# A fast matrix product whose first and fifth products get a PSUM tile each, the first in a single bank

## The chip, the cores and the metric

The kernel runs on one NeuronCore of a Trainium2 chip. The metric is device time in microseconds (us), the median of several runs; lower is better.

## The reference, cut to what matters

```python
def _attn_ref(q, k, v, proj):          # (2, 8, 768, 64) each, proj (64, 6)
    ...
    mask = q_bucket[:, :, :, None] == k_bucket[:, :, None, :]
    scores = scale * np.matmul(q, k.transpose(0, 1, 3, 2))
    scores = np.where(mask, scores, -1000000000.0)
    ...
    return np.matmul(attn, v)
def _moe_ref(x, domain_probs, w1, w2): # x (1536, 512), w1 (4, 512, 1024), w2 (4, 1024, 512)
    p = domain_probs / (domain_probs.sum(-1, keepdims=True) + 1e-09)
    for e in range(E):
        h = np.maximum(x @ w1[e], 0.0)
        out += p[:, e:e + 1] * (h @ w2[e])
```

A hashed attention of two batches is followed by a mixture of four experts on its output. The change touches only the first layer of the experts, `max(x @ w1, 0)`.

## The kernel before, in words

The expert part is cut into 16 **units**, eight for each batch of 768 rows. A unit takes one expert's 512 of 1024 hidden columns: its first layer makes the hidden values (transposed, 128 hidden columns by 384 rows at a time), its second layer multiplies them with `w2` and adds the result to an accumulator. Every fp32 operand is split into a high and a low part, and a product is three matmuls: high by high, high by low, low by high.

Units 0 to 4 use plain products (`unit`). From unit 5 on (`FAST = 5`) there are 11 **fast units** (`unit_fast`, three in batch 0, eight in batch 1). Their first layer is a Strassen-Winograd scheme: four blocks of the result from seven products instead of eight. It is done in two **halves** (`for j in range(2)`, L1096), each with seven products of six matmuls with 384 columns (`product`, L1059 to L1070; its matmuls are L1064, L1067 and L1068). In the text P1 to P7 are the products of a half in the order of the code:

- P1 (L1099) into `pa`; ScalarE then copies `pa` to SBUF as `s1` (L1100).
- P2 (L1104) into `pd`.
- P3 (L1107) into `pb`; VectorE then makes `u2 = pb + s1` and `v1 = pd + u2` (both recorded as L1094, the line of the helper `add`).
- P4 (L1111) is added onto `pa`, whose final value goes to ScalarE (`hh`, L1074) and VectorE (`hl`, L1079) as hidden values.
- P5 (L1116) into `c22`, from which VectorE makes `u3` and `c22 + v1`.
- P6 (L1121) is added onto `pd`, then `pd + u2`.
- P7 (L1127) into `c21`, then `u3 - c21` (L1128).

Each block's hidden values are again an `hh` on ScalarE and an `hl` on VectorE. In between, ScalarE and GpSimd split the `w2` weights (L1049 and L1050), and after the two halves `second_layer` runs six row tiles of 12 matmuls (L783 to L785), each drained by one VectorE instruction (L777 or L813), while the next unit's `w1` operands are made (L1004, L1008, L1013).

PSUM has two pools: `big` gives tiles of two banks (`[P, 2, 512]` fp32, 2 buffers, used by the attention scores too) and `one` gives tiles of one bank (`[P, 512]`, 4 buffers, used by nearly everything else). Before, `pa` and `pd` are the two halves of one `big` tile:

```python
            both = big("mps")
            pa, pd = both[:, 0, :SB], both[:, 1, :SB]
```

The order of instructions on each engine is the order in which the program issues them (`tc.manual_schedule()`); the attention is a generator that is advanced between the steps of the units by costs written into the `yield`s, so that order is fixed before the kernel runs. The tile framework adds the semaphore waits between engines and gives a pool's buffer to a new tile when the old tile's last user is done. In unit 5 the last head's product with `v` (`pv`, L563, in a `one` tile) still runs between P4 and P5 of the first half.

Of the kernel before, what the change touches and what calls it, by code (L numbers as in the profile page):

```python
# [55 lines left out]
def tile_lsh_attention__then__domain_moe(  # L56
# [21 lines left out]
    SB = 384  # L78
# [44 lines left out]
    def pair_tile(shape, name):  # L123
        return pp.tile(shape, F32, tag="pm", name=name, bufs=2)

    def big(name):
        return ps2.tile([P, 2, 512], F32, tag="big", name=name)

    def one(name):
        return ps1.tile([P, 512], F32, tag="one", name=name)  # L130
# [629 lines left out]
    def block(s, f):  # L760
        used = rows_h.setdefault(s, [None, FC])
        if used[1] == FC:
            used[0] = [hp.tile([P, FC, SB], F32R, tag=tag, name=tag) for tag in ("hh", "hl")]
            used[1] = 0
        used[1] += 1
        return tuple(x[:, f] for x in used[0])
# [78 lines left out]
    def drained():  # L845
        while next(att, None) is not None:
            pass
# [132 lines left out]
    def x_ops_late():  # L980
        xop.update(next_ops)
        _, b12, _, b22 = x_blocks(1)
        pair_in("t3", ((stk, "q1"), (stk, "al")))
        t3 = combine(b22, b12, ALU.subtract)
        keep(xop, "t3", t3)
        yield
# [55 lines left out]
    def split_w2_fast(g):  # L1042
        hi = wp.tile([P, KD, HALF], F32R, tag="w2hi", name="w2hi")
        lo = wp.tile([P, KD, HALF], F32R, tag="w2lo", name="w2lo")
        wts[g, 1] = (hi, lo)
        for c in range(0, KD, WC):
            t = staged.pop((g, 1, c))
            for o in range(WC):
                nc.scalar.activation(hi[:, c + o], t[:, o], ACTF.Copy)  # L1049
                nc.gpsimd.tensor_tensor(  # L1050
                    out=lo[:, c + o], in0=t[:, o], in1=hi[:, c + o].bitcast(F32), op=ALU.subtract
                )
            load_w()
            yield

    def unit_fast(b, u, first_u):
        hs = {}

        def product(ps, w, x, j, first):  # L1059
            whi, wlo = w  # L1060
            xh, xl = ([t[k] if isinstance(t, list) else t[:, k] for k in range(KH)] for t in x)
            fs = slice(j * P, (j + 1) * P)
            for kk in range(KH):
                nc.tensor.matmul(  # L1064
                    ps, whi[:, kk, fs], xh[kk], start=first and kk == 0, stop=False, skip_group_check=True
                )
                nc.tensor.matmul(ps, whi[:, kk, fs], xl[kk], start=False, stop=False, skip_group_check=True)  # L1067
                nc.tensor.matmul(  # L1068
                    ps, wlo[:, kk, fs], xh[kk], start=False, stop=kk == KH - 1, skip_group_check=True
                )  # L1070

        def hidden_hi(s, f, src):
            hh, hl = block(s, f)
            nc.scalar.activation(hh, src, ACTF.Relu)  # L1074
            hs[s, f] = (hh, hl)

        def hidden_lo(s, f, src):
            hh, hl = hs[s, f]
            nc.vector.scalar_tensor_tensor(  # L1079
                out=hl, in0=src, scalar=0.0, in1=hh.bitcast(F32), op0=ALU.max, op1=ALU.subtract  # L1080
            )

        def hidden(s, f, src):
            hidden_hi(s, f, src)
            hidden_lo(s, f, src)

        w = wts.pop((first_u + u, 0))
        sp2 = split_w2_fast(first_u + u)
        ma, mb = (pair_tile([P, 2, SB], "mt") for _ in range(2))
        s1, u2, v1, u3 = ma[:, 0], ma[:, 1], mb[:, 0], mb[:, 1]  # L1090
        c21 = None

        def add(out, ps, t):
            nc.vector.tensor_tensor(out=out, in0=ps, in1=t, op=ALU.add)  # L1094

        for j in range(2):  # L1096
            both = big("mps")
            pa, pd = both[:, 0, :SB], both[:, 1, :SB]
            product(pa, w["a11"], xop["b11"], j, True)  # L1099
            nc.scalar.activation(s1, pa, ACTF.Copy)  # L1100
            if j:
                hidden_lo(0, 1 + j, c21)
            yield 1120
            product(pd, w["s1"], xop["t1"], j, True)  # L1104
            yield 1120
            pb = one("mps")[:, :SB]
            product(pb, w["s2"], xop["t2"], j, True)  # L1107
            add(u2, pb, s1)
            add(v1, pd, u2)
            yield 1120  # L1110
            product(pa, w["a12"], xop["b21"], j, False)  # L1111
            hidden(0, j, pa)
            next(sp2, 0)
            yield 1120
            c22 = one("mps")[:, :SB]
            product(c22, w["s3"], xop["t3"], j, True)  # L1116
            add(u3, c22, u2)
            add(c22, c22, v1)
            hidden_hi(1, 2 + j, c22)
            yield 1120  # L1120
            product(pd, w["s4"], xop["b22"], j, False)  # L1121
            add(pd, pd, u2)
            hidden_lo(1, 2 + j, c22)
            hidden_hi(1, j, pd)
            yield 1120
            c21 = one("mps")[:, :SB]
            product(c21, w["a22"], xop["t4"], j, True)  # L1127
            nc.vector.tensor_tensor(out=c21, in0=u3, in1=c21, op=ALU.subtract)  # L1128
            hidden_lo(1, j, pd)
            hidden_hi(0, 2 + j, c21)  # L1130
            yield 1120
        hidden_lo(0, 3, c21)
        for _ in sp2:
            pass
        xo = None
        if b == 0 and u >= EARLY:
            drained()
            xo = early if u + 1 < NU else x_ops_late()
        yield from second_layer(b, u, first_u, hs, wts.pop((first_u + u, 1)), xo)
# [72 lines left out]
```

## Time and profile before

| | |
|---|---|
| median of 3 runs | 772.59 us (772.42 to 772.99) |
| profiled execution: time, span | 772.19 us, 770.4 us |
| busy share of the span: PE, DVE, ACT, POOL | 93%, 64%, 42%, 40% |
| matmuls | 3714 |

The span goes from the first to the last instruction of the profiled execution; about 1.8 us lie around it. PE is TensorE's matmul, PEld its weight load, DVE VectorE, ACT ScalarE, POOL GpSimd, SP the queue that starts the DMAs. Busy time of PE is a modelled figure, since matmuls are pipelined: the distance from one matmul's start to the next one's is the better measure of its pace.

### The profile page before, as it was taken

Reading aid. Unit: us, or ns where it says so; the run is one execution under the profiler, and the core shown is the slowest. Engines: PE = TensorE matmul, PEld = TensorE weight load, DVE = VectorE, ACT = ScalarE, POOL = GpSimd, SP = SyncE. Lnnn points to the kernel's source line nnn. Section 1 sums busy time; section 2 is a strip of 40 time slices with the busy share of each in tenths; the row PEclk is TensorE's granted clock in tenths of the full one; section 3 lists DMA queues with packets and bytes.
Section 4 is the critical chain, followed back from the end, with each engine's and each line's share of the span. In section 5 each row is a group of like instructions: output and inputs, shape, how many; then the busy total and the mean of one; then the engine's idle time right before and its main releaser. Section 6 shows DMA issues by size and latency. Waiting matters only on the chain. (4 is left out here: it accounts for less than half of the span.)

```text
span 770.4 us, 10205 instructions
## 1 busy us (share of the span) xinstructions
PE 714.9 (93%) x3714; PEld 587.0 (76%) x3714; DVE 494.5 (64%) x821; ACT 327.3 (42%) x640; POOL 307.8 (40%) x290
## 2 busy tenths in 40 slices
PE   8999999999999999998888888888898979797988
PEld 6767667978878888886777777777777768686876
DVE  7897988855856656565575756656564646474742
ACT  6887786525534354343333332323232323232330
POOL 6466867243524443253453533323232414141320
PEclk9999999999999999999999999999999999999999
DMA  5325235978978977875111123111112121120202
GB/s 128 73 42 128 52 97 132 246 185 235 248 225 210 231 228 205 244 242 137 54 58 56 54 69 123 55 55 55 55 54 82 47 64 57 53 82 28 83 1 82
DMA packets 90850, 87.77 MB, mean 114 GB/s; under 512 B 53168, under 2 KB 55728, under 8 KB 90800
## 3 DMA queue, kind: packets, MB, share of 16 engines
q1 hardware_dynamic: 89776, 86.80, 40.8%
q8 instruction: 29, 0.48, 0.3%
q10 hardware_dynamic: 1024, 0.33, 0.2%
q14 instruction: 21, 0.17, 0.1%
HBM read 65.04 MB, written 22.07 MB: 113 GB/s over the span
## 5 line engine op out<-in xcount | busy, mean ns | idle before, releaser
L783 PE MATMUL mps<-w2hi,hh 128*128 128x512 f32 (+1 forms) x388 | 151.0, 389 | 0.0
L785 PE MATMUL mps<-w2hi,hl 128*128 128x512 f32 (+1 forms) x388 | 150.4, 388 | 0.0
L784 PE MATMUL mps<-w2lo,hh 128*128 128x512 f32 (+1 forms) x388 | 150.3, 387 | 0.0
L1050 POOL TENSOR_TENSOR w2lo<-ws,w2hi 128x512 fp32r<-128x512 f32 x44 | 56.1, 1296 | 193.8 <-ACT w2hi L1049 110.3
L1064 PE MATMUL mps<-xo,w1hi 128*128 128x384 f32 x260 | 92.5, 356 | 33.2 <-DVE mt L1094 20.9
L1074 ACT ACTIVATE hh<-mps 128x384 fp32r<-128x384 f32 x88 | 43.3, 492 | 150.0 <-PE mps L1068 110.8
L448 DVE TENSOR_SCALAR_CACHE_REDUCE p<-sps 128x768 f32<-128x768 f32 x96 | 90.0, 939 | 17.7 <-PE sps L443 16.0
L777 DVE SCALAR_TENSOR_TENSOR acc<-mps,pe,acc 128x512 f32<-128x512 f32 (+1 forms) x85 | 63.0, 741 | 59.4 <-PE mps L785 59.1
L464 ACT ACTIVATE p<-p,nb 128x768 f32<-128x768 f32 x96 | 89.5, 932 | 23.4 <-DVE p L448 23.0
L1068 PE MATMUL mps<-xo,w1lo 128*128 128x384 f32 x260 | 87.4, 336 | 0.0
L1067 PE MATMUL mps<-xo,w1hi 128*128 128x384 f32 x260 | 87.3, 336 | 0.0
L1064 PEld LDWEIGHTS mps<-xo,w1hi 128*128 128x128 f32 x260 | 48.8, 188 | 49.4 <-DVE mt L1094 26.0
L785 PEld LDWEIGHTS mps<-w2hi,hl 128*128 128x128 f32 x388 | 72.9, 188 | 15.4
L783 PEld LDWEIGHTS mps<-w2hi,hh 128*128 128x128 f32 x388 | 72.9, 188 | 15.4 <-issue 1.2
L784 PEld LDWEIGHTS mps<-w2lo,hh 128*128 128x128 f32 x388 | 72.9, 188 | 13.8
L1094 DVE TENSOR_TENSOR mt<-mps,mt 128x384 f32<-128x384 f32 x66 | 36.8, 557 | 65.7 <-PE mps L1068 64.9
L1079 DVE SCALAR_TENSOR_TENSOR hl<-mps,hh 128x384 fp32r<-128x384 f32 x88 | 48.7, 553 | 44.6 <-ACT hh L1074 42.4
L563 PE MATMUL pv<-pt,tv 128*64 128x384 f32 x288 | 67.1, 492 | 0.0
L1008 POOL TENSOR_TENSOR w1lo<-ws,w1hi 128x512 fp32r<-128x512 f32 x33 | 45.3, 1377 | 41.5 <-issue 14.7
L831 PE MATMUL mps<-xs,w1hi 128*128 128x384 f32 x160 | 54.3, 339 | 0.0
L441 PE MATMUL sps<-ah,q 128*128 128x384 f32 x192 | 53.7, 360 | 0.4 <-DVE p L448 0.4
L833 PE MATMUL mps<-xs,w1lo 128*128 128x384 f32 x160 | 53.8, 336 | 0.0
(136 smaller groups left out, 1332.8 us busy)
## 6 DMA issues: line engine op xcount, KB each, us to landing
ws<-in_moe_w_dram SPq DMA_DIRECT2D x64, 512.0 KB, 3.9
scr<-t SPq DMA_DIRECT2D x16, 1152.0 KB, 8.0
pt<-scr SPq DMA_DIRECT2D x64, 288.0 KB, 6.0
tv<-in_v_dram SPq DMA_DIRECT2D x16, 192.0 KB, 2.9
tqk<-in_q_dram SPq DMA_DIRECT2D x30, 96.0 KB, 3.1
out_dram<-acc SPq DMA_DIRECT2D x11, 256.0 KB, 2.0
tqk<-in_k_dram SPq DMA_DIRECT2D x28, 96.0 KB, 3.3
rdb<-row SPq DMA_DIRECT2D x14, 192.0 KB, 6.5
```

The costliest lines, as they stand in the source:

```text
L448: nc.vector.tensor_scalar(out=two(pt), in0=ps[:, :, :NH], scalar1=MASKED, scalar2=MASKED, op0=ALU.min, op1=ALU.min, accum_out=nb,)
L464: nc.scalar.activation(pt, pt, ACTF.Exp, bias=nb, scale=-1.0, accum_out=dens[b, h, r][:, o : o + 1])
L563: nc.tensor.matmul(dst, vvs[b, h][:, c], pts[b, h, g][c], start=c == 0, stop=c == NT - 1, tile_position=(0, g * D),)
L777: nc.vector.scalar_tensor_tensor(out=acc, in0=ps, scalar=pcol, in1=acc, op0=ALU.mult, op1=ALU.add)
L783: nc.tensor.matmul(ps, hh[:, ts], w2hi[:, f, cs], start=n == 0, stop=False)
L784: nc.tensor.matmul(ps, hh[:, ts], w2lo[:, f, cs], start=False, stop=False)
L785: nc.tensor.matmul(ps, hl[:, ts], w2hi[:, f, cs], start=False, stop=n == FC - 1)
L831: nc.tensor.matmul(ps[:, :SB], w1hi[:, kk, fs], xhi[b, kk][:, sl], start=kk == 0, stop=False)
L1050: nc.gpsimd.tensor_tensor(out=lo[:, c + o], in0=t[:, o], in1=hi[:, c + o].bitcast(F32), op=ALU.subtract)
L1064: nc.tensor.matmul(ps, whi[:, kk, fs], xh[kk], start=first and kk == 0, stop=False, skip_group_check=True)
L1067: nc.tensor.matmul(ps, whi[:, kk, fs], xl[kk], start=False, stop=False, skip_group_check=True)
L1068: nc.tensor.matmul(ps, wlo[:, kk, fs], xh[kk], start=False, stop=kk == KH - 1, skip_group_check=True)
```

## The change

`pa` becomes a tile of one bank out of the pool `one`; `pd` is the first half of a `big` tile, whose second half is left unused. No instruction is added, removed or reordered by the diff, and no operand changes its shape.

```diff
         for j in range(2):
-            both = big("mps")
-            pa, pd = both[:, 0, :SB], both[:, 1, :SB]
+            pa, pd = one("mps")[:, :SB], big("mps")[:, 0, :SB]
             product(pa, w["a11"], xop["b11"], j, True)
             nc.scalar.activation(s1, pa, ACTF.Copy)
```

## Rows read from the trace of the kernel before

**Rows 1.** The page: instructions and busy shares, and the granted clock in 40 slices.
```profile
PE 714.9 (93%) x3714; PEld 587.0 (76%) x3714; DVE 494.5 (64%) x821; ACT 327.3 (42%) x640; POOL 307.8 (40%) x290
...
PEclk9999999999999999999999999999999999999999
```

**Rows 2.** Busy time by stretch: fast units' first layers, without unit 5's 364.53:368.55.
```profile
core 0: us, PE busy (x) PEld busy (x) DVE busy (x) ACT busy (x) POOL busy (x), PEclk, DMA share, GB/s
356.53:364.53 8.00, 4.83 (x26) 3.94 (x24) 4.79 (x8) 1.76 (x3) 1.66 (x1) 1.00 0.98 242
368.55:381.94 13.39, 11.37 (x62) 10.41 (x61) 7.72 (x15) 4.71 (x10) 2.24 (x2) 1.00 0.11 39
...
730.07:750.43 20.36, 16.21 (x85) 14.29 (x84) 9.52 (x18) 6.25 (x13) 4.79 (x4) 1.00 0.00 1
sum 226.47, PE 178.28 PEld 157.26 DVE 109.68 ACT 69.69 POOL 57.93; mean PE 14.86 PEld 13.10 DVE 9.14 ACT 5.81 POOL 4.83
```

**Rows 3.** Busy time by stretch: attention beside plain units, and one second layer.
```profile
120.00:344.70 224.70, 224.70 (x1185) 187.28 (x1184) 149.47 (x248) 101.40 (x199) 93.92 (x87) 1.00 0.82 221
...
713.73:730.07 16.34, 16.34 (x74) 13.52 (x73) 12.09 (x16) 4.96 (x9) 5.49 (x5) 1.00 0.29 98
```

**Rows 4.** Line L1064, whole span: what PE and PEld together waited for.
```profile
  DVE mt L1094: 64.3, 44
  ACT mt L1100: 40.5, 44
  DVE hl L1079: 9.5, 21
```

**Rows 5.** Timeline of PE, last first layer: first matmuls of P1, P2, P3, P4, P6, P7, P1.
```profile
730.07 0.34 PE L1064 MATMUL mps<-xo,w1hi 128*128 128x384 f32 x1
...
731.91 0.44 PE L1064 MATMUL mps<-xo,w1hi 128*128 128x384 f32 x1 [0.64 <-ACT mt L1100]
...
733.06 0.34 PE L1064 MATMUL mps<-xo,w1hi 128*128 128x384 f32 x1
...
735.58 0.45 PE L1064 MATMUL mps<-xo,w1hi 128*128 128x384 f32 x1 [1.31 <-DVE mt L1094]
...
738.06 0.45 PE L1064 MATMUL mps<-xo,w1hi 128*128 128x384 f32 x1
...
739.21 0.34 PE L1064 MATMUL mps<-xo,w1hi 128*128 128x384 f32 x1
...
740.25 0.34 PE L1064 MATMUL mps<-xo,w1hi 128*128 128x384 f32 x1
```

**Rows 6.** Timeline of ACT, the same first layer.
```profile
731.37 0.49 ACT L1100 ACTIVATE mt<-mps 128x384 f32<-128x384 f32 x1 [3.66 <-PE mps L1068]
736.92 0.49 ACT L1074 ACTIVATE hh<-mps 128x384 fp32r<-128x384 f32 x1 [5.07 <-PE mps L1068]
737.31 1.14 ACT L1049 ACTIVATE w2hi<-ws 128x512 fp32r<-128x512 f32 x2
```

**Rows 7.** Timeline of DVE, around the same first layer.
```profile
728.22 0.68 DVE L1008 TENSOR_TENSOR w1lo<-wc,w1hi 128x512 fp32r<-128x512 f32 x1
730.27 0.75 DVE L777 SCALAR_TENSOR_TENSOR acc<-mps,pe,acc 128x512 f32<-128x512 f32 x1 [1.37 <-PE mps L785]
734.37 1.15 DVE L1094 TENSOR_TENSOR mt<-mps,mt 128x384 f32<-128x384 f32 x2 [3.35 <-PE mps L1068]
737.45 0.56 DVE L1079 SCALAR_TENSOR_TENSOR hl<-mps,hh 128x384 fp32r<-128x384 f32 x1 [1.92 <-ACT hh L1074]
...
751.11 1.20 DVE L1079 SCALAR_TENSOR_TENSOR hl<-mps,hh 128x384 fp32r<-128x384 f32 x2
```

**Rows 8.** Timeline of POOL, second half of the same first layer.
```profile
748.19 2.54 POOL L1050 TENSOR_TENSOR w2lo<-ws,w2hi 128x512 fp32r<-128x512 f32 x2 [7.57 <-ACT w2hi L1049]
```

**Rows 9.** Timeline of SP at the start of unit 5.
```profile
354.95 1.79 SPq L545 DMA_DIRECT2D pt<-scr  x4
```

**Rows 10.** DMA issues, 354.9 to 366.5 us: count, KB each, median us to landing.
```profile
pt<-scr SPq DMA_DIRECT2D x4, 288.0 KB, 6.0
```

## The prediction, made before the changed kernel ran

> **What bounds the kernel now.** I read the page first: PE is busy 93% of the span and its granted clock is at the upper level, 2.4 GHz, in all 40 slices [rows 1]. So TensorE is the bound, and a change can gain no more than the time in which TensorE stands still. The view by stretch says where that is. Between 120 and 344.7 us PE is busy 100% of the time, and in a second layer it is too: 16.34 of 16.34 us [rows 3]. The first layers of the fast units are different: the last one takes 20.36 us with 16.21 busy, and the eleven together take 226.47 us, without the 4.02 us that the attention's last `pv` product takes out of unit 5 [rows 2].
>
> What the stops wait for stands in the view of the line of the products' first matmul: VectorE's additions 44 times, ScalarE's copy `s1` 44 times, `hl` 21 times [rows 4]. PE and its weight load are counted apart there, so that is 22 stops each (11 units by 2 halves) behind the additions and the copy, and 21 behind `hl`. The timeline shows which products stop [rows 5]. P7 starts at 739.21 and the next P1 at 740.25, so a product that nothing holds up takes 1.04 us and a half of seven would take 7.28. It takes 740.25 − 730.07 = 10.18. The 2.90 us too many lie so:
>
> - P1 to P2: 1.84 us instead of 1.04. P2 starts at 731.91; the copy of `pa` ends at 731.37 + 0.49 = 731.86 [rows 6].
> - P2 to P3: 1.15, so 0.11 more after the restart.
> - P3 to P4: 2.52, so 1.48 more. P4 starts at 735.58; the pair `u2`, `v1` ends at 734.37 + 1.15 = 735.52 [rows 7].
> - P4 to P6: 2.48 instead of 2.08, so 0.40, of which 0.11 is P4's restart. P6 starts at 738.06; `hl` of `pa` ends at 737.45 + 0.56 = 738.01 [rows 7].
> - P6 to P7: 1.15, again 0.11 of restart.
>
> Each stop ends 0.05 or 0.06 us after an instruction on the *other* half of the tile `both`. P2 writes `pd` and waits for a reader of `pa`; P4 writes `pa` and waits for `v1`, which reads `pd`; P6 writes `pd` and waits for `hl`, which reads `pa`. None of the three pairs shares a value. I conclude that waits are kept for the tile as a whole.
>
> **The change part by part.** It adds and removes no instruction. With `pa` and `pd` in two tiles, P2 has nothing to wait for but its buffer; P4 must wait only for the copy of `pa`, P6 only for `v1`.
>
> *The gain.* Eleven first layers of 14.56 us are 160.16, against 226.47: 66.31 us [rows 2, 5].
>
> *What comes late next.* I lay a half out anew, P1 at 0. A reader starts 1.31 us after its product's first matmul (734.37 − 733.06) [rows 5, 7]. Copy `s1`: 1.31 to 1.80, and P4 starts at 3.12. `u2` and `v1`: P3 at 2.08, so 3.39 to 4.54; P6 starts at 5.20 and needs `v1`, with 0.6 us to spare. ScalarE's `hh` of `pa` is at 4.43, its weight pair ends at 4.43 + 0.39 + 1.14 = 5.96 [rows 6], `hl` of `pa` starts at 4.96 (737.45 − 736.92 later). Behind it come seven more VectorE instructions of about 0.56 us, some waiting for P5, P6 and P7 and for `hh`: `u3` at 5.47, `c22 + v1` until 6.5, its `hh` until 7.0 and its `hl` until 7.6; carried on, 9.3 for the last `hl`. The next half's `u2` is due at 7.28 + 3.39 = 10.67, and VectorE is busy only 9.52 us in a first layer [rows 2]. So no product waits, and I cost the rest of the half at nothing; if `v1` came late after all, the wait at P6 returns, up to its present 0.40 a half, 8.8 us in all.
>
> *The second layer* starts at 14.56. GpSimd's second pair of `w2lo` runs 748.19 to 750.73 [rows 8]; P4 of that half started 735.58 + 10.18 = 745.76, so in the new half, with P4 at 10.40, it ends at 15.37. The last piece is wanted at about 14.56 + 7 matmuls of 16.34 / 72 = 0.227 us [rows 3], 16.15: 0.8 us to spare. The weight load that waits for it goes out 0.5 us later against the second layer than before; the next unit's last operand is done 1.2 us before P1 now (728.22 + 0.68 against 730.07) [rows 3, 7] and is wanted by P6, so I take nothing for that.
>
> *Buffers.* P1 now draws from the four `one` tiles: 14 a unit instead of 12. If they go round in turn, P1 of the second half gets the buffer of the first half's `pa`, free at 5.5, and P1 of a unit that of the second layer's third row tile, long drained. Nothing.
>
> *Unit 5.* After P4, at 356.53 + 4.16 = 360.69, comes `pv` instead of at 364.53 [rows 2]. Its `pt` loads were issued until 354.95 + 1.79 = 356.74 [rows 9] and land 6.0 us later by the median [rows 10], 362.74. So it would wait: 0 at the least, 3.84 at the most (it ran at 364.53 before); I take 2.1 from the landing. The `pv` tile also stands in the ring of `one` tiles, and in turn its buffer falls to P3 of the second half. Its two copies come behind `s1`: at like shapes [rows 6, 7] 1.80 + 0.49 + 0.56 = 2.85 after P1 against 2.08, with the restart 0.9 us. Bounds are 0 and 0.9, since the ring is only my reading; I take 0.9.
>
> *Sum*: 66.3 − 2.1 − 0.9 = 63.3 us. From the profiled execution 772.19 − 63.3 = 708.9; its median is 0.4 above it, so 709.3.
>
> *A rule against it.* The rows say that P2 waits for a reader of another half of its tile. The Trainium skill ("PSUM — Partial Sum Buffer", section "PSUM bank collisions raise a hardware error") has engines kept apart by bank and quadrant; two halves of 512 fp32 are two banks, so by that rule nothing between them would have had to wait, the change would remove no wait, and the time would stay at 772.6. The trace disagrees with it as a description of this program: 22 stops behind the copy.
>
> **The rivals.**
>
> 1. *The stop is not the shared tile's*, and stays: 772.6. For it: `hl` of SBUF tiles is tracked in parts (the second layer begins at 750.43 [rows 2] while VectorE writes other parts of the same `hl` at 751.11 [rows 7]), so tiles need not be tracked whole. Against it: three stops a half, each 0.05 us after a reader of the other half of `both`, and no other instruction ends there. 6%.
>
> 2. *Too few one-bank buffers*: P1 gets a buffer freed late. The latest that can be meant are, at the unit's start, the sixth row tile, whose drain ends at 731.02 [rows 7], 1.0 us after P1's start, and, in the second half, `c22`, whose `hl` ends at 7.6 in the layout above, 0.4 after P1's 7.28. With 0.11 of restart each that is 1.6 us a unit, 17.6 in all: 727. Against it: a second layer takes its six row tiles from the same ring, and PE never stops in it [rows 3]. 7%.
>
> 3. *Slower: the clock.* If TensorE without its stops fell to its lower level, 1.2 GHz, in the first layers, each would cost 14.56 us more. From 63.3 / 14.56 = 4.3 of the eleven on this eats the gain; with all eleven the time is 709.3 + 160 = 869. Against it: 224.7 us without a stop at a granted clock of 1.00 [rows 3]. 2%.
>
> 4. *P6 keeps its wait* because VectorE runs behind: 709.3 + 8.8 = 718. It lies inside the forecast's range.
>
> **How the numbers follow.** The forecast, including number 4, has 85%. Its own range goes from 706.3 (all of the 66.3 us: 772.6 − 66.3) to 718. I widen it by a microsecond at each end, 705 to 719, which leaves out rivals 1 to 3 (15%) and some odd case. About 0.2% is what a measurement here can tell from no change. Faster: 85 + 7 = 92%; the same 6%; slower 2%.
>
> **What would show it.** By stretch, first layers of 14.6 us in batch 1 and second layers of 16.3 still; on L1064 no idle time behind `s1`, the additions or `hl` beyond a few us; PE busy near 99%. A stop at P6 behind the additions would say that `v1` is late, one at P1 behind L777 or `hl` that the ring is too small, one before `pv` in unit 5 that `pt` had not landed. The prediction is wrong if P2 still starts 0.05 us after the copy, or if a new stop appears at the second layer's first row tile.

## The result and the profile after

| | before | after |
|---|---|---|
| median of 4 runs | 772.50 us | 712.18 us (710.60 to 713.37) |
| ratio, 95% interval | | 0.9217 (0.9198 to 0.9237) |
| profiled execution: time, span | 772.19, 770.4 us | 713.37, 711.6 us |

The changed kernel is 7.8% faster. The forecast of 709.3 us was 2.9 us too low, with the time inside its range. (The "fifth" product of the title is P2 in the numbering of the text: `pd` takes P2, and P6 is added onto it.)

The page of the changed kernel, its parts on busy time and on the granted clock:

```profile
PE 701.8 (99%) x3714; PEld 592.3 (83%) x3714; DVE 498.6 (70%) x821; ACT 327.7 (46%) x640; POOL 307.7 (43%) x290
...
PEclk9999999999999999999999999999999999999999
```

Beside [rows 1], the work is the same, 3714 matmuls, and PE has gone from 93% to 99% of a span that is 58.8 us shorter. Of these, 45.7 us are idle time of TensorE (770.4 − 714.9 before, 711.6 − 701.8 after). The other 13.1 are modelled busy time around the stops: before a stop a matmul counts its whole 0.34 us, and behind one 0.44, while in a run only 0.17 us lie between two starts.

Busy time by stretch in the changed kernel: unit 5's first layer up to the end of P4, its `pv` part and its rest; the first layers of units 6, 7 and 8 and the last one, the sum of these and the seven in between, and a second layer. The columns are those of [rows 2].

```profile
358.02:362.34 4.32, 4.32 (x25) 3.99 (x23) 4.25 (x8) 1.76 (x3) 1.68 (x1) 1.00 0.85 200
362.34:371.61 9.27, 6.62 (x26) 2.76 (x25) 1.06 (x2) 1.64 (x3) 2.50 (x2) 0.82 0.65 172
371.61:382.17 10.56, 10.56 (x62) 10.56 (x62) 7.72 (x15) 4.72 (x10) 1.85 (x2) 1.00 0.12 44
398.53:413.43 14.90, 14.89 (x85) 14.57 (x84) 11.44 (x20) 6.99 (x14) 7.41 (x6) 1.00 0.17 57
429.79:444.46 14.67, 14.67 (x85) 14.59 (x84) 10.75 (x19) 6.34 (x14) 8.68 (x7) 1.00 0.25 79
460.83:475.39 14.56, 14.56 (x86) 14.56 (x85) 9.74 (x19) 6.26 (x13) 4.39 (x4) 1.00 0.46 142
...
677.08:691.64 14.56, 14.56 (x86) 14.56 (x84) 9.54 (x18) 6.25 (x13) 4.38 (x4) 1.00 0.00 1
sum 170.22, PE 167.57 PEld 162.93 DVE 111.74 ACT 71.48 POOL 57.19; mean PE 12.89 PEld 12.53 DVE 8.60 ACT 5.50 POOL 4.40
...
660.75:677.08 16.33, 16.33 (x74) 13.51 (x73) 12.45 (x16) 4.95 (x9) 5.90 (x5) 1.00 0.30 98
```

The first layers of batch 1 take 14.56 or 14.57 us where [rows 2] has 20.36: seven products of 1.04 us twice, with PE busy all the time. The second layer has kept its 16.33. Most of what is left over stands in unit 5, between P4 and P5; units 6 and 7 keep 0.34 and 0.11 us.

The line of the products' first matmul, the same question as [rows 4], and the timeline of PE in the last first layer, P1, P2, P3, P4 and P6 (beside [rows 5]):

```profile
  issue: 0.6, 1
  ACT mt L1099: 0.3, 1
```

```profile
677.08 0.34 PE L1064 MATMUL mps<-xo,w1hi 128*128 128x384 f32 x1
...
678.12 0.34 PE L1064 MATMUL mps<-xo,w1hi 128*128 128x384 f32 x1
...
679.16 0.34 PE L1064 MATMUL mps<-xo,w1hi 128*128 128x384 f32 x1
...
680.20 0.34 PE L1064 MATMUL mps<-xo,w1hi 128*128 128x384 f32 x1
...
682.28 0.34 PE L1064 MATMUL mps<-xo,w1hi 128*128 128x384 f32 x1
```

All the stops behind the copy, the additions and `hl` are gone, but for one of 0.3 us behind the copy, in unit 6. In the same stretch ScalarE and VectorE read the tiles while TensorE runs on (the copy `s1` is now on L1099, one line being gone):

```profile
678.38 0.49 ACT L1099 ACTIVATE mt<-mps 128x384 f32<-128x384 f32 x1 [3.49 <-PE mps L1068]
```

```profile
680.47 1.15 DVE L1094 TENSOR_TENSOR mt<-mps,mt 128x384 f32<-128x384 f32 x2 [2.44 <-PE mps L1068]
```

ScalarE reads `pa` from 678.38 to 678.87 while P2, begun at 678.12, writes `pd`. The pair `u2`, `v1` ends at 681.62, and P6, which needs it, starts at 682.28: 0.66 us to spare.

Unit 5 in the changed kernel: the timeline of PE at `pv`, that of SP before it, and the busy time right behind the stop.

```profile
362.42 0.86 PE L563 MATMUL pv<-pt,tv 128*64 128x384 f32 x2
365.93 5.75 PE L563 MATMUL pv<-pt,tv 128*64 128x384 f32 x22 [2.65 <-DMA pt<-scr]
371.61 0.45 PE L1064 MATMUL mps<-xo,w1hi 128*128 128x384 f32 x1
```

```profile
356.04 0.34 SPq L478 DMA_DIRECT2D row<-rd  x1
356.48 1.79 SPq L545 DMA_DIRECT2D pt<-scr  x4
```

```profile
366.00:368.00 2.00, 2.00 (x8) 0.94 (x10) 0.00 (x0) 1.15 (x2) 0.44 (x1) 0.59 0.94 281
368.00:370.00 2.00, 2.00 (x10) 0.99 (x8) 0.00 (x0) 0.00 (x0) 2.00 (x2) 0.56 0.03 9
370.00:372.00 2.00, 2.00 (x12) 0.92 (x9) 0.00 (x0) 0.00 (x0) 0.06 (x1) 1.00 0.28 92
```

Two matmuls of `pv` have their data, the third has to wait for `pt` until 365.93. Behind the stop the granted clock is 0.59 and 0.56 on the mean of two microseconds, so near the lower of TensorE's two levels, and the other 22 matmuls take 5.68 us up to P5. (A slice of the page is 17.8 us long, so its row of nines does not show this.) From P4's end to P5 pass 9.27 us, where `pv` took 4.02 before. The Trainium skill ("TensorE: Matmul & The Clock Gate", section "HAM oscillation — how this bites in real kernels") says that TensorE, left without work for a while, comes back at half its clock; this trace agrees, with 0.59 and 0.56. The runs e3, e4 and g3 below stop at the same place and keep 1.00.

### The profile page after: what moved, and what is told of

The parts are those of the page before. It is cut to its first block, busy times and chain, and to the rows that moved or that the text cites. A ratio compares the mean times of both kernels' runs of the same rounds, so it can differ in the third digit from the quotient of the medians.

```text
span 711.6 us, 10184 instructions
## 1 busy us (share of the span) xinstructions
PE 701.8 (99%) x3714; PEld 592.3 (83%) x3714; DVE 498.6 (70%) x821; ACT 327.7 (46%) x640; POOL 307.7 (43%) x290
## 4 chain that ended last, share of the span: by engine, by line
PE 87%; DMA 4%; DVE 3%; POOL 2%; issue 2%; ACT 1%; SPq 1%; POOLq 0%; DVEq 0%
PE mps L783 12%; PE mps L785 12%; PE mps L784 12%; PE pv L563 8%; PE mps L1064 7%; PE mps L1068 7%; PE mps L1067 7%; PE sps L443 4%; PE sps L441 4%; PE ptps L509 4%; PE mps L831 3%; PE mps L833 3%; PE mps L832 3%; DMA pt<-scr 3%; DMA ws<-in_moe_w_dram 1%
## 5 line engine op out<-in xcount | busy, mean ns | idle before, releaser
L448 DVE TENSOR_SCALAR_CACHE_REDUCE p<-sps 128x768 f32<-128x768 f32 x96 | 90.1, 939 | 17.8 <-PE sps L443 16.2
L1064 PE MATMUL mps<-xo,w1hi 128*128 128x384 f32 x260 | 87.4, 336 | 0.0
L1067 PE MATMUL mps<-xo,w1hi 128*128 128x384 f32 x260 | 87.3, 336 | 0.0
L563 PE MATMUL pv<-pt,tv 128*64 128x384 f32 x288 | 70.5, 505 | 2.9 <-DMA pt<-scr 2.9
L563 PEld LDWEIGHTS pv<-pt,tv 128*64 128x64 f32 x288 | 26.4, 140 | 36.9 <-issue 33.5
L1004 ACT ACTIVATE w1hi<-wc 128x512 fp32r<-128x512 f32 x44 | 27.4, 630 | 58.9 <-DVE wc L1013 58.9
```

The lines of the kernel that those rows point to most:

```text
L448: nc.vector.tensor_scalar(out=two(pt), in0=ps[:, :, :NH], scalar1=MASKED, scalar2=MASKED, op0=ALU.min, op1=ALU.min, accum_out=nb,)
L563: nc.tensor.matmul(dst, vvs[b, h][:, c], pts[b, h, g][c], start=c == 0, stop=c == NT - 1, tile_position=(0, g * D),)
L1064: nc.tensor.matmul(ps, whi[:, kk, fs], xh[kk], start=first and kk == 0, stop=False, skip_group_check=True)
```

## The experiments

Theory: the framework keeps waits for a PSUM tile as a whole, so that each of the three stops is one read of the other half; and what is missing from the forecast is the late landing of `pt` in unit 5. Rivals: the single bank or its pool is what helped; the stops are one chain; the buffers go in turn and are too few; `pv` waits for something else. Each group of runs shares a chip with runs of the kernel before; across groups the ratios are compared. Ratios have their 95% interval.

| run | edit | median us | ratio to before |
|---|---|---|---|
| e1 | change, `pa` in a two-bank tile too | 717.80 | 0.9273 (0.9256 to 0.9290) |
| e2 | before, P4 in its own tile | 732.80 | 0.9466 (0.9444 to 0.9487) |
| e3 | before, `s1` not from `pa` | 753.39 | 0.9738 (0.9717 to 0.9758) |
| e4 | change, `u2` three times | 724.18 | 0.9361 (0.9342 to 0.9380) |
| f1 | change | 712.00 | 0.9182 (0.9157 to 0.9207) |
| f2 | change, `pt` loads before the row store | 707.62 | 0.9127 (0.9103 to 0.9151) |
| f3 | change, `pv` one step later | 707.43 | 0.9127 (0.9103 to 0.9152) |
| f4 | before, `pt` loads before the row store | 773.32 | 0.9985 (0.9970 to 1.0000) |
| g1 | change, `u2` twice | 714.04 | 0.9233 (0.9220 to 0.9247) |
| g2 | `pa` two-bank, `pd` single | 712.11 | 0.9207 (0.9192 to 0.9222) |
| g3 | both in single banks | 711.30 | 0.9200 (0.9183 to 0.9216) |

### e1: two tiles, but no single bank

```diff
-            pa, pd = one("mps")[:, :SB], big("mps")[:, 0, :SB]
+            pa, pd = big("mps")[:, 0, :SB], big("mps")[:, 0, :SB]
```

> The first product's tile comes from the two-bank pool too, so pa and pd are two tiles but no single-bank buffer is used. If the stops came from sharing one tile: first layers near 14.6 us and a time near that of the change, 712, plus what two buffers in place of one-bank ones cost: P2 of the second half gets the buffer of the first half's pd, whose last reader (hl) ends about 8.5 us after P1 where P2 could start at 8.32, so 0.2 to 0.4 us in each of 11 units, 2 to 4 us, 714 to 716. If it was the single bank or the one-bank pool that helped: the three stops of each half are back and the time is 772.

717.8 us. The question on L1064 in e1:

```profile
  DVE hl L1079: 4.3, 11
  issue: 0.6, 1
  ACT mt L1099: 0.5, 2
```

The weight load of P2 in the last unit's second half, and the stretch of that first layer:

```profile
688.98 0.19 PEld L1064 LDWEIGHTS mps<-xo,w1hi 128*128 128x128 f32 x1 [0.39 <-DVE hl L1079]
```

```profile
680.42:695.33 14.91, 14.84 (x86) 14.51 (x84) 9.54 (x18) 6.25 (x13) 4.38 (x4) 1.00 0.01 2
```

The three stops stay away, without any single bank, so what counts is that there are two tiles. New are 11 stops, one a unit, behind `hl` of the first half's `pd`: the buffer wait that was expected. The 4.3 us are idle time of the weight load, which otherwise runs ahead; the matmul itself comes 0.24 us late, and its restart costs 0.11. So a first layer takes 14.91 us instead of 14.56, 0.35 more, and the eleven 3.9. `pv`'s stop is also 0.9 us longer here than in the change (3.52 us of named idle time against 2.65). Together that is 4.8 us, within the distance to the change (0.9273 against 0.9182 to 0.9217, so 4.3 to 7.0 us). The 717.8 us are above the 714 to 716 of the expectation, which left `pv` out and did not know that the kernel before would take 773.9 us on this chip.

### e2 and e3: the stops one by one

```diff
-            product(pa, w["a12"], xop["b21"], j, False)
-            hidden(0, j, pa)
+            pc = one("mps")[:, :SB]
+            product(pc, w["a12"], xop["b21"], j, True)
+            hidden(0, j, pc)
```

> The kernel before, with P4 in a one-bank tile of its own instead of on top of pa (the sum of P1 and P4 is left out). P4 and P6 then have no reader of the other half to wait for; P2 still has. If the stops are the shared tile's and add up: only P2's stop is left, 0.80 + 0.11 us in 22 halves, 20 us more than the change: 732. If the stops are one chain, so that with two of them gone the third grows or goes too: 712 or 750 and more.

```diff
-            nc.scalar.activation(s1, pa, ACTF.Copy)
+            nc.scalar.activation(s1, accs[b if u else 0, 0][:, :SB], ACTF.Copy)
```

> The kernel before, with the copy s1 reading an accumulator in SBUF instead of pa (so s1 has other data). Only P2's stop goes: 20 us less than before, 752.5, with P4 still 0.05 us behind v1 and P6 behind hl of pa. If the stops were not the shared tile's but a matter of TensorE's pace, P2 would still stop and the time would stay at 772.

732.8 and 753.4 us, the kernel before on the same chip 773.9. The question on L1064 (44 is again 22 stops, each counted on PE and on its weight load), in e2:

```profile
  ACT mt L1100: 43.2, 44
  issue: 0.6, 1
```

and in e3:

```profile
  DVE mt L1094: 64.9, 44
  DVE hl L1079: 9.5, 21
  issue: 0.6, 1
```

Each edit takes away exactly the stops that it should and leaves the others near the size of [rows 4]. P4's and P6's stops together are worth 773.9 − 732.8 = 41.1 us and P2's 773.9 − 753.4 = 20.5, against 43.8 (22 times 1.48 + 0.40 + 0.11) and 20.0 (22 times 0.80 + 0.11) by the prediction's terms. Those terms are the last unit's. By the starts of the first matmuls in all 22 halves of the kernel before it is 43.4 and 22.9, because in units 5, 6 and 7 the first half's P1 to P2 takes 3.08, 2.77 and 2.43 us and not 1.84; the two make the forecast's 66.3.

Both prices are net of a loss in unit 5. In e3 `pv` has to wait for `pt` too, and P4 to P5 takes 2.9 us more than before (8.16 against 5.28):

```profile
366.14 4.06 PE L563 MATMUL pv<-pt,tv 128*64 128x384 f32 x22 [2.04 <-DMA pt<-scr]
```

In e2 the granted clock falls for a time (see the last section). The change loses at `pv` as well. So that the two prices make 61.6, between the 60.6 and 63.3 us that the change's two ratios (0.9217 and 0.9182) make of 773.9, shows to within some 3 us that the stops add up; they are not one chain.

### e4 and g1: how much room VectorE has

```diff
             add(u2, pb, s1)
+            add(u2, pb, s1)
+            add(u2, pb, s1)
             add(v1, pd, u2)
```

> The change, with the addition u2 done three times instead of once. It measures how much room P6 has: v1 ends 4.54 us after P1 in the changed kernel and P6 starts at 5.20. Two more additions of 0.56 us put v1 at 5.65: P6 stops for 0.5 us and 0.1 of restart in 22 halves, about 13 us, 725 (one stop of L1064 behind the additions in each half). If VectorE has more room than that layout says, or P6 does not depend on v1 at all: 712.

724.2 us, some 12 more than the change. In e4 the timeline of PE shows P6 of both halves, and that of DVE the additions before the first of them:

```profile
692.05 0.44 PE L1064 MATMUL mps<-xo,w1hi 128*128 128x384 f32 x1 [0.41 <-DVE mt L1094]
700.00 0.44 PE L1064 MATMUL mps<-xo,w1hi 128*128 128x384 f32 x1 [0.40 <-DVE mt L1094]
```

```profile
689.66 2.33 DVE L1094 TENSOR_TENSOR mt<-mps,mt 128x384 f32<-128x384 f32 x4 [2.44 <-PE mps L1068]
```

The additions end at 691.99 and P6 starts 0.06 later: P6 does depend on `v1`, and two more additions overrun the room. One more (g1, the edit with one added line):

> The change, with the addition u2 done twice. One more addition of 0.56 us puts v1's end at 5.10 after P1, and P6 starts at 5.20: no stop, 712 to 713. If P6 has less room than the layout says, a stop of up to 0.1 us and its restart in 22 halves: 714 to 717.

714.0 us. The timelines of g1 around P6 of the last unit's first half, and the weight load of P6 in g1 and, below it, in the change:

```profile
682.42 0.43 PE L1064 MATMUL mps<-xo,w1hi 128*128 128x384 f32 x1
683.03 0.34 PE L1064 MATMUL mps<-xo,w1hi 128*128 128x384 f32 x1
```

```profile
680.61 1.74 DVE L1094 TENSOR_TENSOR mt<-mps,mt 128x384 f32<-128x384 f32 x3 [2.44 <-PE mps L1068]
```

```profile
682.41 0.19 PEld L1064 LDWEIGHTS mps<-xo,w1hi 128*128 128x128 f32 x1
682.11 0.19 PEld L1064 LDWEIGHTS mps<-xo,w1hi 128*128 128x128 f32 x1
```

The additions end at 682.35, and P6 starts at 682.42, which is also when it is due. It doesn't come late, but its first three matmuls take 0.61 us instead of 0.52: the weight load, which in the change starts 0.17 us ahead of its matmul (at 682.11 for 682.28), starts only 0.01 ahead. In the 20 halves of units 6 to 15 P6 takes 1.7 us more in all, nearly the 1.9 us between g1 and g2, which ran beside each other. The second reading of the expectation is the one that came true, and the room is 0.6 us, as laid out, less what a running start needs.

### g2 and g3: are there enough single banks?

```diff
-            pa, pd = one("mps")[:, :SB], big("mps")[:, 0, :SB]
+            pa, pd = big("mps")[:, 0, :SB], one("mps")[:, :SB]   # g2
+            pa, pd = one("mps")[:, :SB], one("mps")[:, :SB]      # g3
```

> The change the other way round: pa in the two-bank pool, pd in a single bank. The two are two tiles again, so the three stops stay away. If the one-bank pool gives its four buffers strictly in turn, pd of the second half gets that of the first half's pd and P2 waits for its hl as in the run with two two-bank tiles, 0.5 us a unit: 717. If the pool gives whichever buffer was freed first, P2 finds one free: 712.

> Both pa and pd in single banks: five tiles a half out of four buffers. It tests the rival that there are too few one-bank buffers. If a buffer that was freed first is given first, each product finds one that is free by then: 712, within 2. If the buffers go strictly in turn, each half shifts the turn by one and some product meets a buffer whose hl is still to come: 716 to 730, with stops of L1064 behind hl.

712.1 and 711.3 us, within the spread of the change. The question on L1064 in g3, with five one-bank tiles a half out of four buffers:

```profile
  issue: 0.6, 1
  DVE hl L1079: 0.5, 1
  ACT w1hi L1004: 0.2, 1
```

One stop behind a reader, 0.5 us of the weight load's time, in the whole kernel. The four buffers suffice even for five tiles, and g2 shows none of e1's 11 stops: the pool does not go strictly in turn. Which buffer it gives was not read from the runs. That also answers the 0.9 us that I had set for the buffer of `pv` in unit 5, which never came.

### f1 to f4: the stop before pv

In f2 and f4 the last head's `pt` loads are issued one step of the attention earlier, before instead of behind the store of its row of reciprocals; in f3 `pv` itself is moved by one step.

```diff
+                last = i in (n - 1 + LAG_Y - 1, n - 1 + LAG_Y)
+                if i == n - 1 + LAG_Y:
+                    return None
-                j = i - LAG_Y
+                j = n - 1 if last else i - LAG_Y
```

```diff
     def v_lags(b, h):
+        if (b, h) == (B - 1, H - 1):
+            return (8,)
```

> The changed kernel once more, beside the next three: 712.2, with the stop before the attention's last pv product in unit 5 and, in most executions, a lower granted clock behind it.

> The change, with the loads of pt for the last head issued one step earlier, ahead of the store of its row of sums, which stands before them in the DMA queue and waits for VectorE. If the stop of 3.5 us before pv and the slow pv behind it (9.3 us from P4's end to P5 instead of 4.0) come from the late loads: both go, 5.2 us less, 707, in every execution alike. If pv waits for something else, or the loads take as long as before from wherever they start: 712.

> The change, with the last pv product one step of the attention later, some products further on in unit 5. If the landing of pt at about 366 us is what pv waits for, PE finds other products to do meanwhile: 707 again. If pv's lateness costs the steps behind it (its copies, the scaling, the operands of batch 1): more than 709.

> The kernel before, with the same earlier loads as in the change's variant. In it pv ran at 364.53 without a stop, so the loads were hidden: 772.5, within 0.5 us. A gain of some us here would say that the late loads cost time before the change too.

712.0, 707.6, 707.4 and 773.3 us. In f2, whose lines behind the edit are three further down, the timelines of SP and of PE:

```profile
347.58 1.75 SPq L545 DMA_DIRECT2D pt<-scr  x4
355.34 0.34 SPq L478 DMA_DIRECT2D row<-rd  x1
```

```profile
361.72 4.09 PE L563 MATMUL pv<-pt,tv 128*64 128x384 f32 x24
365.74 0.44 PE L1067 MATMUL mps<-xo,w1hi 128*128 128x384 f32 x1
```

In the changed kernel the loads went out at 356.48, right behind the row store at 356.04, which stood at the head of the DMA queue and had waited 15.2 us for VectorE's reciprocal. In front of it they go out at 347.58, almost nine us earlier, and `pv` runs through in 4.02 us at the full clock. f3 leaves the loads where they were and gives PE other products meanwhile; its `pv`:

```profile
365.40 4.09 PE L563 MATMUL pv<-pt,tv 128*64 128x384 f32 x24
```

Either way the stop and the lower clock behind it are gone, and 4.4 to 4.6 us with them (5.2 were expected). On the kernel before the same edit gives 0.9985 (0.9970 to 1.0000), not clearly different from no change: there `pv` runs without a stop with the late loads too [rows 2], so they were hidden under the stops that the change removes. f2 and f3 beat both kernels, the change by 0.6%.

The lower clock did not come in every execution. Of the eight of the change (result and f1), the two with a mean granted clock of 1.000 took 710.60 and 710.59 us, the six with 0.997 or 0.998 took 711.72 to 713.37. In g3's profiled execution the clock stayed at the upper level (1.00 between 366 and 370 us); its 22 matmuls then take 4.05 us:

```profile
364.50 4.05 PE L563 MATMUL pv<-pt,tv 128*64 128x384 f32 x22 [1.99 <-DMA pt<-scr]
```

## Why the prediction was right, point by point

- **The bound.** Right. TensorE's idle time in the fast units' first layers was the whole prize, and only `pv`'s wait in unit 5 took back more than a microsecond of it.
- **The cause of the stops.** Right, and shown: two tiles without a single bank do it (e1), each stop can be taken away alone (e2, e3), and their prices are those read from the first matmuls' starts. The rule of the Trainium skill that was weighed against the change ("PSUM — Partial Sum Buffer", section "PSUM bank collisions raise a hardware error") has engines kept apart by bank and quadrant; the trace after agrees, since TensorE writes `pd` in one bank from 678.12 on while ScalarE reads `pa` in another from 678.38 to 678.87, without a wait. So the wait lay in the program's semaphores, which the framework sets, and it followed the two-bank tile as one. Why it does so here and follows an SBUF tile like `hl` in parts, no run shows. Rival 1 is out.
- **What comes late next.** Right. The forecast had P6 0.6 us behind `v1`; 0.66 is left by the profile, and e4 and g1 show where it ends. The first layers have the forecast 14.56 us, and the second layer never stops.
- **Buffers.** No stop in the change, as forecast. The turn by which I argued is wrong (g2, g3, and `pv`'s 0.9 us that did not come); so rival 2 is out.
- **Unit 5's `pv`.** The mechanism was forecast, the size was not: 9.27 − 4.02 = 5.25 us lost instead of 2.1. Of it about 3.2 are the stop (from 362.42 to 365.93, less two matmuls of about 0.17), 1.7 the lower clock behind it (22 matmuls in 5.75 us, against 4.05 in g3, whose clock stayed up), and the rest is the restart. The stop was put too short by some 1.1 us: 356.74 + 6.0 took the median of the loads, but `pv` needs the last part of them, which landed 7.7 us after the last issue (358.27 to 365.93). The lower clock behind a stop was not in the sum at all.
- **The clock (rival 3).** In the change it fell once, in unit 5, for some 4 us, and not in the first layers as such; from unit 8 on, with PE busy without a pause, it kept 1.00.
- **Small terms.** Unit 6 keeps 0.34 us: its `s1` comes late from ScalarE, which makes an operand for batch 1 just before, and P4, which truly needs it, starts 0.17 late and restarts for 0.11. Unit 7's 0.11 has no stop; in f1 both units keep only 0.07.

The sum from P1 of unit 5 to the end: before 770.4 − 356.53 = 413.9 us, after 711.6 − 358.02 = 353.6, so 60.3 gained. The prize of 66.3, less 5.25 at `pv`, 0.45 in units 6 and 7 and 0.16 in each of the two other parts of unit 5, is 60.3. Against the forecast's 63.3 that is 3.0 less: `pv` cost 3.15 more and the small terms 0.77, while the 0.9 for `pv`'s buffer did not come. This last error made the miss smaller by luck. The span is shorter by 58.8 and not by 60.3 because unit 5 began at 358.02 instead of 356.53, in code that is the same. In the other profiled executions, of either kernel and its variants, it begins between 356.8 and 357.9, so nothing shows that the change moved it.

## What to carry to other kernels

When an engine restarts a few hundredths of a microsecond after another engine has read something it does not use, look for a tile that the two share: here splitting one tile into two took 7.8% off, with no instruction made faster. Then lay the shorter schedule out anew and ask of every load and every sum that used to be hidden in the old pauses whether it is still in time; here four loads that stood behind a store in the queue cost some 4.5 us of the gain. What room is left can be measured by doubling a cheap instruction on the engine that is next.

## What the runs showed of the hardware that was not expected

Behind a single stop of about 3.2 us in the change TensorE's granted clock was 0.59 and 0.56 for the next 4 us, which cost half as much again. The length of the stop alone does not decide it. Before the same instruction the clock fell behind 2.41 us of named idle time in g2 and 2.65 in the change, and it stayed at 1.00 behind 1.99 in g3, 2.04 in e3 and 2.29 in e4. But it also fell in e2's profiled execution behind a stop of only 1.88 us, the one before P2 in unit 5, and behind 1.85 us at the same place the kernel before kept 1.00. First e2, then the kernel before, each with P2's first matmul and a stretch behind it:

```profile
361.01 0.44 PE L1064 MATMUL mps<-xs,w1hi 128*128 128x384 f32 x1 [1.88 <-ACT mt L1100]
...
362.00:364.00 2.00, 2.00 (x8) 2.00 (x8) 0.00 (x0) 0.00 (x0) 0.00 (x0) 0.50 1.07 213
```

```profile
359.61 0.45 PE L1064 MATMUL mps<-xs,w1hi 128*128 128x384 f32 x1 [1.85 <-ACT mt L1100]
...
360.00:362.00 2.00, 1.96 (x12) 1.64 (x10) 0.25 (x1) 0.00 (x0) 0.00 (x0) 1.00 1.07 221
```

What else decides it stays open.

And an operand that comes exactly in time is not free: in g1 P6 starts when it is due, but its weight load can't run ahead, and 0.07 to 0.10 us are lost in each of 20 halves.
